# Grouped-query attention and a SwiGLU block for one decode step: K and V of two batches per load, a softmax maximum through TensorE, the FFN behind the last V, and W_O in long runs

## The chip, the cores and the metric

The kernel runs on one core of a Trainium2 chip. The core has five engines with instruction queues of their own: TensorE (PE, matmuls, with its weight loads shown as PEld), VectorE (DVE), ScalarE (ACT), GpSimd (POOL) and SyncE (SP, which here only issues transfers). They meet through semaphores. Data goes from memory (HBM) to the on-chip SBUF by DMA, split over 16 DMA engines; matmul results land in PSUM, in eight banks of 2 KB per partition.

The metric is the device time of one execution in microseconds, the median of several runs. The profile is one execution, recorded by the hardware profiler; its span runs from the first to the last instruction and is a little shorter than that run's time.

## The reference

Four sequences (B = 4), one new token each, D = 512. There are 32 query heads on 8 key/value heads (REP = 4 queries share one K and V), head size 128, and attention sees the last W = 4096 positions of a cache of 16384. All data is bf16.

```python
xn = layernorm(x)                                   # [4, 1, 512]
q  = (xn @ wq).reshape(4, 1, 32, 128)               # wq [512, 4096]
k  = repeat(k_cache[:, :, Sk - W:, :], 4, axis=1)   # cache [4, 8, 16384, 128]
v  = repeat(v_cache[:, :, Sk - W:, :], 4, axis=1)
p  = softmax(q . k * 128 ** -0.5)                   # over the 4096 positions
o  = (p . v).reshape(4, 1, 4096)
ffn = (silu(xn @ w_gate) * (xn @ w_up)) @ w_down    # [512, 1792], [512, 1792], [1792, 512]
out = x + o @ wo + ffn                              # wo [4096, 512]
```

K and V in the window are 33.6 MB each, W_Q and W_O 4.2 MB each, the three FFN weights 1.8 MB each: 81 MB that are read once.

## The kernel before

The kernel is written engine by engine: each engine's program is one list, and the order in the list is the order in which that engine works. What sets the order between engines are the semaphore waits that stand in the lists.

**Loads.** SP's list holds all large loads in one order (lines 182 to 194): W_Q in two halves, K of the first pair, W_gate, W_up, W_down, V of the first pair, then K and V of the other pairs in turn, and W_O in four pieces (`WO_CUTS`). A pair is one batch and one key/value head; there are 32. K and V of a pair are 1 MB each, laid out so that a partition holds 32 consecutive positions, which is one run of 8 KB. There are four slots for K and four for V. A load into a used slot waits until the old content has been consumed: K for the transposes (`s_tr`), V for the products with the probabilities (`s_pv`). SP waits in order, so whatever stands behind a waiting load waits too.

**Start.** ACT's queue loads x. VectorE, with ScalarE for the square and the square root, makes the layer norm (lines 217 to 226: `st_sum`, `xc`, `st_var`, `st_rstd`, `xn`). TensorE transposes xn, and makes q in 128 matmuls (line 291). GpSimd meanwhile fills constants: the identity, ones, a selection pattern, and zeros or ones in buffers that are read before they are first written (P, QT, one slot of VB), and signals `s_const` after the last of them. Then gate, up, exp, silu and down of the FFN run (lines 295 to 308), and their sum with x is kept in `y0`.

**Loop.** For each pair TensorE transposes 32 blocks of K (line 317, four groups of eight into four PSUM banks), VectorE copies each group to SBUF (`kT`, line 236), TensorE multiplies them with q to scores (line 325), ScalarE takes the exponential (line 210, with no maximum subtracted), and TensorE forms the denominators by a matmul on ones (line 335) and the products with V (line 338), which run one pair behind. VectorE reduces the denominators, inverts them and scales the output (lines 242 to 246). In TensorE's list a pair is: transposes of this pair, products with V for the pair before, scores of this pair.

**End.** The scaled outputs are permuted by matmuls on the pattern `sel` and copies (`permute`, `perm_copy`) into the layout in which W_O was loaded, in runs of 4 KB. 64 matmuls of 256 columns on W_O (line 354) add to `ps_acc`, into which y0 was put first. VectorE copies the sum to bf16, and two stores write it out.

Of the kernel before, what the change touches and what calls it, by code (L numbers as in the profile page):

```python
# [3 lines left out]
BF16 = mybir.dt.bfloat16  # L4
# [6 lines left out]
def bass_parallel_sum__sliding_block_cached__swiglu_ffn__decode_kernel(  # L11
# [18 lines left out]
    NT = W // 128  # L30
# [3 lines left out]
    NPAIR = B * HKV  # L34
    NSL = 4
    NG = 4
    KVN = NT * Dh
    PN = NT * REP
    WIDE = 64
    PS = PN + WIDE  # L40
    SCALE = float(Dh) ** -0.5
    EPS = 1e-5

# [3 lines left out]
    WQ = sb("wq_sb", [128, NC, HQ * Dh], BF16)  # L47
# [3 lines left out]
    WO = sb("wo_sb", [128, HKV, REP, D], BF16)  # L51
    KB = sb("kbuf", [128, NSL * NT * Dh], BF16)
    VB = sb("vbuf", [128, NSL * NT * Dh], BF16)
    KT = sb("kT", [128, 2 * NT * 128], BF16)
    P = sb("p", [128, 2 * PS], BF16)
    ident = sb("ident", [128, 128], BF16)
    ones = sb("ones", [128, 128], BF16)
    sel = sb("sel", [128, REP, REP, 32], BF16)
# [9 lines left out]
    QT = sb("qT", [128, HKV + 4, B, REP], BF16)  # L68
    den = sb("den", [128, REP], FP32)
    OT = sb("oT", [128, 1 + NPAIR, REP], BF16)  # L70
    OP = sb("oP", [128, REP, HKV, B], BF16)
# [4 lines left out]
    y0 = sb("y0", [B, D], FP32)  # L76
    I4w = sb("i4w", [B, 64], FP32)
# [3 lines left out]
    ps_kt = [ps("ps_kt%d" % s, [128, 512], FP32) for s in range(4)]  # L81
    ps_S = ps("ps_s", [128, 512], FP32)
    ps_O = ps("ps_o", [128, 512], FP32)
    ps_m = ps("ps_m", [128, 512], FP32)
# [3 lines left out]
    O_ps = ps_O[:, 0:REP]  # L88
    O_wide = ps_O[:, 0:WIDE]
    den_ps = ps_O[:, 128:128 + NT * REP]  # L90
    gate_ps = ps_m[:, 0:NF * B]
    up_ps = ps_m[:, 64:64 + NF * B]
    perm_ps = ps_m[:].rearrange("p (e k b h) -> p h e k b", e=REP, k=HKV, h=REP)
    q_ps = ps_acc[:, 0:HQ * B]
    down_ps = ps_acc[0:B, :]
    xT_ps = ps_m[:, 128:128 + NC * B]
# [4 lines left out]
    d_wq = [sem("d_wq%d" % h) for h in range(2)]  # L101
# [4 lines left out]
    WO_CUTS = (0, 3, 6, 7, 8)  # L106
    d_wo = [sem("d_wo%d" % q) for q in range(len(WO_CUTS) - 1)]
    s_xc = sem("s_xc")
    s_ss = sem("s_ss")
    d_k = [sem("d_k%d" % s) for s in range(NSL)]  # L110
    d_v = [sem("d_v%d" % s) for s in range(NSL)]
    s_const = sem("s_const")
# [6 lines left out]
    s_gu = sem("s_gu")  # L119
    s_ex = sem("s_ex")  # L120
    s_guT = sem("s_guT")
    s_tr = sem("s_tr")
    s_ev = sem("s_ev")
    s_sc = sem("s_sc")
    s_p = sem("s_p")
    s_pv = sem("s_pv")
    s_nrm = sem("s_nrm")
    s_pm = sem("s_pm")
    s_pc = sem("s_pc")
    s_acc = sem("s_acc")  # L130
    s_dn = sem("s_dn")
    s_y0 = sem("s_y0")
# [4 lines left out]
    wq_ap = A_wq.rearrange("(p c) n -> p c n", c=NC)  # L137
# [3 lines left out]
    wo_ap = A_wo.rearrange("(k p e) n -> p k (e n)", k=HKV, e=REP)  # L141
    ds = bass.ds

    def kv_ap(cache, i):
        return cache[i % B, i // B, Sk - W:, :].rearrange("(p t) d -> p t d", t=NT)

    with nc.Block() as block:

        @block.gpsimd
        def _(eng):  # L150
            eng.memset(ident[:], 0.0)
            eng.memset(I4[:], 0.0)
            eng.memset(I4w[:], 0.0)
            eng.memset(ones[:], 1.0)
            eng.drain()
            eng.affine_select(I4[:], I4[:], pattern=[[-1, B]], compare_op=ALU.not_equal,
                              fill=1.0, base=0, channel_multiplier=1)
            eng.affine_select(ident[:], ident[:], pattern=[[-1, 128]], compare_op=ALU.not_equal,
                              fill=1.0, base=0, channel_multiplier=1)
            eng.drain()  # L160
            eng.tensor_copy(I4w[:, 0:B], I4[:])
            for h in range(REP):
                eng.tensor_copy(sel[:, :, h, :], ident[:].rearrange("p (m e) -> p e m", e=REP))
            eng.memset(P[:], 1.0)
            eng.memset(QT[:, HKV:], 0.0)
            eng.memset(VB[:, (NSL - 1) * KVN:], 0.0).then_inc(s_const, 1)

        @block.sync
        def _(eng):
            def load_k(i):  # L170
                if i >= NSL:
                    eng.wait_ge(s_tr, NG * (i - NSL + 1))
                eng.dma_start(KB[:, i % NSL * KVN:(i % NSL + 1) * KVN].rearrange("p (t d) -> p t d", t=NT), kv_ap(A_k_cache, i)).then_inc(d_k[i % NSL], 16)  # L173

            def load_v(i):
                if i == NSL - 1:
                    eng.wait_ge(s_pv, 1)
                if i >= NSL:
                    eng.wait_ge(s_pv, i - NSL + 2)
                eng.dma_start(VB[:, i % NSL * KVN:(i % NSL + 1) * KVN].rearrange("p (t d) -> p t d", t=NT), kv_ap(A_v_cache, i)).then_inc(d_v[i % NSL], 16)  # L180

            eng.dma_start(WQ[:, 0:2], wq_ap[:, 0:2]).then_inc(d_wq[0], 16)
            eng.dma_start(WQ[:, 2:4], wq_ap[:, 2:4]).then_inc(d_wq[1], 16)
            load_k(0)
            eng.dma_start(WG[:], wg_ap).then_inc(d_wg, 16)  # L185
            eng.dma_start(WU[:], wu_ap).then_inc(d_wu, 16)
            eng.dma_start(WD[:], wd_ap).then_inc(d_wd, 16)
            load_v(0)
            for i in range(1, NPAIR):
                load_k(i)  # L190
                load_v(i)
            for n in range(len(d_wo)):
                a, b = WO_CUTS[n], WO_CUTS[n + 1]
                eng.dma_start(WO[:, a:b].rearrange("p k e n -> p k (e n)"), wo_ap[:, a:b]).then_inc(d_wo[n], 16)  # L194
# [5 lines left out]
        def _(eng):  # L200
# [5 lines left out]
            eng.wait_ge(s_gu, 1)  # L206
            eng.activation(ex[:], gate_ps.rearrange("p (t b) -> p t b", b=B), ACT.Exp, scale=-1.0).then_inc(s_ex, 1)  # L207
            for j in range(NPAIR):
                eng.wait_ge(s_sc, j + 1)
                eng.activation(P[:, j % 2 * PS:j % 2 * PS + PN], ps_S[:, 0:PN], ACT.Exp, scale=SCALE).then_inc(s_p, 1)  # L210
# [4 lines left out]
        def _(eng):  # L215

# [11 lines left out]
            eng.tensor_copy(XnT[:], xT_ps.rearrange("p (c b) -> p c b", b=B)).then_inc(s_xnT, 1)  # L228
            eng.wait_ge(s_q, 1)
            eng.tensor_copy(QT[:, 0:HKV], q_ps.rearrange("p (k h b) -> p k b h", k=HKV, b=B)).then_inc(s_nrm, 1)  # L230
            eng.engine_nop().then_inc(s_ev, 3)

            def evac(i):
                for g in range(NG):
                    eng.wait_ge(s_tr, i * NG + (g + 1))
                    eng.tensor_copy(KT[:, ds((i & 1) * KVN + 1024 * g, 1024)],  # L236
                                    kt_ps[g].rearrange("p a b -> p (a b)")).then_inc(s_ev, 1)


            def norm(j1):  # L240
                eng.wait_ge(s_pv, j1 + 1)
                eng.tensor_reduce(den[:], den_ps.rearrange("p (t h) -> p h t", h=REP), AX.X, ALU.add)  # L242
                eng.drain()
                eng.reciprocal(den[:], den[:])  # L244
                eng.drain()
                eng.tensor_tensor(OT[:].rearrange("p j h -> p (j h)")[:, ds(j1 * REP, REP)], O_ps, den[:],  # L246
                                  ALU.mult).then_inc(s_nrm, 1)

            def ffn():
                eng.wait_ge(s_ex, 1)  # L250
                eng.tensor_scalar(ex[:], ex[:], 1.0, None, ALU.add)  # L251
                eng.drain()
                eng.reciprocal(ex[:], ex[:])  # L253
                eng.drain()
                eng.tensor_tensor(gs[:], gate_ps.rearrange("p (t b) -> p t b", b=B), ex[:], ALU.mult)
                eng.drain()
# [151 lines left out]
```

## Time and profile before

| | us |
|---|---|
| median of 3 runs (lowest, highest) | 199.16 (198.95, 200.85) |
| the profiled run | 199.1 |
| its span | 197.1 |
| PE busy in the span | 150.2 |
| PE weight loads busy | 138.2 |
| DVE busy | 107.6 |
| ACT busy | 13.9 |
| POOL busy | 6.1 |
| K load, issue to landing (median of 32) | 16.2 |
| V load, issue to landing (median of 32) | 14.1 |

Busy time is a sum over instructions, and matmuls overlap in PE's pipeline, so PE's 150.2 is not time at its full rate. The page divides the span in 40 slices of 4.9 us and gives for each how busy the engines and the DMA engines were and how many GB/s moved. The time from a load's issue to its landing includes the time that it stood in the queue behind others.

### The profile page before, as it was taken

What the parts mean: (1) busy time and instruction counts of PE and PEld (TensorE: products, weight loads), DVE (VectorE), ACT (ScalarE), POOL (GpSimd) and SP (SyncE); (2) the same over time, 40 slices, a digit from 0 to 9 for tenths busy, and PEclk for the clock granted to TensorE, in tenths of its full rate; (3) what the DMA queues carried; (4) which work ended last, traced back from release to release, by engine and by line L of the source; (5) the groups of instructions that cost most, each with busy time, mean ns of one, the idle gap of its engine ahead of it and who ended that gap; (6) DMA issues with size and microseconds to landing.
All of it is one profiled execution on the core that took longest, in us unless ns stands there. A gap on an engine that the chain in (4) does not pass through costs nothing.

```text
span 197.1 us, 8105 instructions
## 1 busy us (share of the span) xinstructions
PE 150.2 (76%) x3471; PEld 138.2 (70%) x3471; DVE 107.6 (55%) x248; ACT 13.9 (7%) x39; POOL 6.1 (3%) x18
## 2 busy tenths in 40 slices
PE   0080778888888888888888888888888888888864
PEld 0080662788888878887777777877787777777742
DVE  5510001766677777666666666666666666666730
ACT  2520000001000000000000000000000000000000
POOL 8400000000000000000000000000000000000000
PEclk9999999999999999999999999999999999999999
DMA  6999999999999999999999999999999999999990
GB/s 224 429 422 433 434 424 422 426 424 426 422 422 429 427 426 429 426 427 427 429 429 431 427 426 426 427 426 429 427 426 429 426 429 426 431 429 422 418 416 37
DMA packets 11054, 81.11 MB, mean 412 GB/s; under 512 B 1180, under 2 KB 1192, under 8 KB 2216
## 3 DMA queue, kind: packets, MB, share of 16 engines
q1 hardware_dynamic: 11032, 81.01, 97.7%
q8 instruction: 6, 0.10, 0.2%
q10 hardware_dynamic: 16, 0.01, 0.0%
HBM read 81.01 MB, written 0.00 MB: 411 GB/s over the span
## 4 chain that ended last, share of the span: by engine, by line
DMA 61%; PE 26%; SPq 4%; DVE 4%; issue 3%; DVEq 0%; ACT 0%
DMA kbuf<-in_A_k_cache_dram 40%; PE ps_kt L317 13%; DMA wu_sb<-in_B_w_up_dram 11%; DMA wo_sb<-in_A_wo_dram 9%; PE ps_s L325 4%; PE ps_o L338 3%; DVE kT L236 3%; SPq L194 3%; PE ps_acc L307 2%; PE ps_m L299 2%; SPq L180 1%; PE ps_acc L354 0%; SPq L185 0%; DVE ex L253 0%; SPq L173 0%
## 5 line engine op out<-in xcount | busy, mean ns | idle before, releaser
L236 DVE COPY kT<-ps_kt 128x1024 bf16 x128 | 79.5, 683 | 45.2 <-PE ps_kt L317 45.1
L317 PE MATMUL ps_kt<-ident,kbuf 128*128 128x128 bf16 x1024 | 62.6, 219 | 6.8 <-DMA kbuf<-in_A_k_cache_dram 6.7
L317 PEld LDWEIGHTS ps_kt<-ident,kbuf 128*128 128x128 bf16 x1024 | 57.4, 98 | 9.6 <-issue 7.9
L325 PE MATMUL ps_s<-qT,kT 128*128 x1024 | 35.3, 192 | 15.8 <-DVE kT L236 15.8
L325 PEld LDWEIGHTS ps_s<-qT,kT 128*128 128x128 bf16 x1024 | 31.7, 97 | 19.4 <-issue 19.4
L338 PE MATMUL ps_o<-p,vbuf 128*128 128x64 bf16 x1056 | 36.3, 193 | 0.6 <-issue 0.6
L338 PEld LDWEIGHTS ps_o<-p,vbuf 128*128 128x128 bf16 x1056 | 34.0, 98 | 0.6 <-issue 0.6
L210 ACT ACTIVATE p<-ps_s 128x128 bf16<-128x128 f32 x32 | 8.9, 278 | 148.8 <-PE ps_s L325 148.8
L242 DVE TENSOR_REDUCE den<-ps_o 128x4 f32<-128x128 f32 x33 | 9.2, 279 | 0.9 <-PE ps_o L338 0.9
L283 PE MATMUL ps_m<-i,xn 4*128 4x4 f32 x4 | 0.6, 254 | 10.4 <-DVE xn L226 10.4
L246 DVE TENSOR_TENSOR oT<-ps_o,den 128x4 f32 (+1 forms) x33 | 5.3, 162 | 5.3 <-issue 5.2
L299 PE MATMUL ps_m<-xnT,wg_sb 128*128 128x4 bf16 x56 | 3.5, 199 | 6.2 <-DMA wg_sb<-in_B_w_gate_dram 6.2
L283 PEld LDWEIGHTS ps_m<-i,xn 4*128 4x128 f32 x4 | 0.6, 208 | 10.4 <-issue 10.4
L299 PEld LDWEIGHTS ps_m<-xnT,wg_sb 128*128 128x128 bf16 x56 | 3.4, 159 | 6.2 <-DMA wg_sb<-in_B_w_gate_dram 6.2
L251 DVE TENSOR_SCALAR ex<-ex 128x56 f32<-128x56 f32 x1 | 0.2, 191 | 13.9 <-ACT ex L207 13.9
L335 PE MATMUL ps_o<-p,ones 128*128 128x128 bf16 x33 | 7.2, 219 | 0.0
L244 DVE RECIPROCAL den<-den 128x4 f32<-128x4 f32 x33 | 5.9, 177 | 2.4
L307 PE MATMUL ps_acc<-wd_sb,guT 128*4 128x512 bf16 x14 | 4.9, 527 | 1.7 <-DVE guT L257 1.7
L354 PE MATMUL ps_acc<-wo_sb,oP 128*4 128x256 bf16 x64 | 4.2, 272 | 2.0 <-DMA wo_sb<-in_A_wo_dram 2.0
L307 PEld LDWEIGHTS ps_acc<-wd_sb,guT 128*4 128x4 bf16 x14 | 1.5, 110 | 4.7 <-issue 2.5
L354 PEld LDWEIGHTS ps_acc<-wo_sb,oP 128*4 128x4 bf16 x64 | 2.5, 84 | 3.1 <-DMA wo_sb<-in_A_wo_dram 1.6
L220 DVE TENSOR_SCALAR xc<-x_sb,st_sum 4x512 f32<-4x512 bf16 x1 | 4.4, 4381 | 0.1
(43 smaller groups left out, 36.6 us busy)
## 6 DMA issues: line engine op xcount, KB each, us to landing
kbuf<-in_A_k_cache_dram SPq DMA_DIRECT2D x32, 1024.0 KB, 16.2
vbuf<-in_A_v_cache_dram SPq DMA_DIRECT2D x32, 1024.0 KB, 14.1
wq_sb<-in_A_wq_dram SPq DMA_DIRECT2D x2, 2048.0 KB, 9.6
wo_sb<-in_A_wo_dram SPq DMA_DIRECT2D x2, 1536.0 KB, 19.1
wg_sb<-in_B_w_gate_dram SPq DMA_DIRECT2D x1, 1792.0 KB, 18.9
wu_sb<-in_B_w_up_dram SPq DMA_DIRECT2D x1, 1792.0 KB, 22.5
wd_sb<-in_B_w_down_dram SPq DMA_DIRECT2D x1, 1792.0 KB, 26.3
wo_sb<-in_A_wo_dram SPq DMA_DIRECT2D x2, 512.0 KB, 20.1
```

What stands on the lines that cost most here:

```text
L194: eng.dma_start(WO[:, a:b].rearrange("p k e n -> p k (e n)"), wo_ap[:, a:b]).then_inc(d_wo[n], 16)
L210: eng.activation(P[:, j % 2 * PS:j % 2 * PS + PN], ps_S[:, 0:PN], ACT.Exp, scale=SCALE).then_inc(s_p, 1)
L236: eng.tensor_copy(KT[:, ds((i & 1) * KVN + 1024 * g, 1024)], kt_ps[g].rearrange("p a b -> p (a b)")).then_inc(s_ev, 1)
L242: eng.tensor_reduce(den[:], den_ps.rearrange("p (t h) -> p h t", h=REP), AX.X, ALU.add)
L244: eng.reciprocal(den[:], den[:])
L299: last = mm(o[:, t * B:(t + 1) * B], w[:].rearrange("p c (m t) -> p c t m", t=NF)[:, c, t, :], XnT[:, c, :], start=(w is WG and t == 0 and ...
L307: last = mm(down_ps, guT[:, t, :], WD[:, t, :], start=(t == 0), stop=(t == NF - 1))
L317: last = eng.transpose(kt_ps[g][:, k, :], KB[:, a:a + 128], ident[:])
L325: last = mm(ps_S[:, REP * t:REP * t + WIDE], KT[:, a:a + 128], q)
L335: mm(den_ps, ones[:], P[:, p:p + PN])
L338: last = mm(O_wide, VB[:, a:a + 128], P[:, p + REP * t:p + REP * t + WIDE], start=(t == 0), stop=(t == NT - 1))
L354: last = mm(ps_acc[64 * n:64 * n + B, 0:256], OP[:, e, q, :], WO[:, q, e, 256 * n:256 * n + 256], start=False, stop=(q == HKV - 1 and e == ...
```

## The change

- K and V are loaded for two batches of one key/value head at once: 16 loads of 2 MB each in place of 32 of 1 MB. A partition holds 64 consecutive positions of one batch, a run of 16 KB; even partitions belong to the one batch and odd ones to the other. There are two slots each in place of four.
- Scores of both batches are computed together, eight columns per block. A matmul of rank two (`mask`) puts -1e30 where a partition and a column belong to different batches.
- A maximum is subtracted: VectorE reduces the scores over the blocks (`row_max`), TensorE transposes that (`max_rows`), VectorE reduces it and puts it on a diagonal (`shift`), and a matmul adds it, negated, to all 512 columns of scores. The exponential follows that.
- In TensorE's list an iteration is now: first half of the transposes, transposed maximum of the iteration before, second half of the V products of two iterations before, first half of the scores, shift, second half of the transposes, first half of the V products of the iteration before, second half of the scores.
- W_Q is one load. W_down stays early; W_gate and W_up come behind the last V, and the whole FFN runs there. Its down product, x and W_O add up in the same PSUM bank, without y0.
- W_O is loaded with 32 rows per partition, in pieces of 16, 10, 4 and 2 KB per partition. The outputs are brought into that layout by four transposes, a copy and four matmuls on a pattern `rep`.
- Constants change with all that: GpSimd clears more buffers, among them three quarters of VB in place of a quarter, and signals `s_const` in two steps.

```diff
+    ND = B * HKV // 2
+    C = 2 * REP
+    NT = 2 * W // 128
+    HT = NT // 2
...
-    wo_ap = A_wo.rearrange("(k p e) n -> p k (e n)", k=HKV, e=REP)
+    wo_ap = A_wo.rearrange("(p c) n -> p c n", c=NO)
...
-    def kv_ap(cache, i):
-        return cache[i % B, i // B, Sk - W:, :].rearrange("(p t) d -> p t d", t=NT)
+    def kv_ap(cache, d):
+        b0 = d % 2 * 2
+        return cache[b0:b0 + 2, d // 2, Sk - W:, :].rearrange("b (q t) d -> q b (t d)", t=NT)
...
+            eng.memset(QZ[:], 0.0)
+            eng.drain()
+            eng.engine_nop().then_inc(s_const, 1)
             eng.memset(P[:], 1.0)
-            eng.memset(QT[:, HKV:], 0.0)
-            eng.memset(VB[:, (NSL - 1) * KVN:], 0.0).then_inc(s_const, 1)
+            eng.memset(VB[:, HKN:], 0.0)
+            eng.drain()
+            eng.engine_nop().then_inc(s_const, 1)
+            eng.engine_nop().then_inc(d_v[1], 16)
...
+            def load_k(d):
+                if d >= 2:
+                    eng.wait_ge(s_tr, 2 * NG * (d - 1))
+                eng.dma_start(KB[:, d % 2 * KVN:(d % 2 + 1) * KVN], kv_ap(A_k_cache, d)).then_inc(d_k[d % 2], 16)
+
+            def load_v(d):
+                eng.wait_ge(s_pv, d + 1)
+                eng.dma_start(VB[:, d % 2 * KVN:(d % 2 + 1) * KVN], kv_ap(A_v_cache, d)).then_inc(d_v[d % 2], 16)
+
+            eng.dma_start(WQ[:], wq_ap).then_inc(d_wq, 16)
             load_k(0)
+            load_k(1)
+            eng.dma_start(WD[:], wd_ap).then_inc(d_wd, 16)
+            load_v(0)
+            for d in range(2, ND):
+                load_k(d)
+                load_v(d - 1)
+            load_v(ND - 1)
             eng.dma_start(WG[:], wg_ap).then_inc(d_wg, 16)
             eng.dma_start(WU[:], wu_ap).then_inc(d_wu, 16)
...
+            with eng.Fori(0, ND // 2) as r:
+                for b in range(2):
+                    row_max(1 - b, 2 * r + (b + 1))
+                    evac(0, 4 * NG * r + 2 * NG * b)
+                    shift(2 * r + (b + 1))
+                    norm(2 * r + (b + 1), b, r)
+                    evac(1, 4 * NG * r + (2 * NG * b + NG))
...
+            def mask(bank):
+                return mm(ps_S[bank][:].rearrange("p (t c) -> p t c", c=C), mkr[:],
+                          mkc[:].rearrange("j (o c) -> j o c", o=1).to_broadcast([2, NT, C]), start=True)
...
+            def shift(bank, n):
+                eng.wait_ge(s_dg, n)
+                mm(ps_S[bank][:].rearrange("p (t c) -> p t c", c=C), ones[0:C, :],
+                   Dg[:].rearrange("j (o c) -> j o c", o=1).to_broadcast([C, NT, C])).then_inc(s_sh, 1)
...
+            eng.wait_ge(s_const, 2)
+            eng.wait_ge(s_qz, 1)
+            mm(ps_O[:, 0:256], ones[:], P[:, 0:256], start=True)
+            mask(1).then_inc(s_sc, 1)
...
+                    eng.wait_ge(d_k[b], r * 16 + 16)
+                    transposes(0, ev, b)
+                    max_rows(n)
+                    pv(b, 1, n)
+                    scores(0, ev, b, q)
+                    shift(1 - b, n)
+                    transposes(1, ev + NG, b)
+                    pv(1 - b, 0, (r * 16 + 16, n))
+                    scores(1, ev + NG, b, q)
+            max_rows(ND + 1)
+            pv(0, 1, ND + 1)
+            shift(1, ND + 1)
...
+            pv(1, 0, (8 * ND + 16, ND + 1))
+            pv(1, 1, None)
+            up_gate(WG, gate_ps, s_gate, d_wg)
...
+            up_gate(WU, up_ps, s_up, d_wu)
+            for n in range(2):
+                mm(ps_acc[64 * n:64 * n + 64, 0:256], I4w[:], X[:, 256 * n:256 * n + 256], start=True)
             eng.wait_ge(s_guT, 1)
             eng.wait_ge(d_wd, 16)
             for t in range(NF):
...
+                for n in range(2):
+                    mm(ps_acc[64 * n:64 * n + B, 0:256], guT[:, t, :], WD[:, t, 256 * n:256 * n + 256])
+            eng.wait_ge(s_op, 1)
+            for c in range(NO):
+                if c in WO_CUTS:
+                    eng.wait_ge(d_wo[WO_CUTS.index(c)], 16)
+                for n in range(2):
+                    last = mm(ps_acc[64 * n:64 * n + B, 0:256], OP[:, c, :], WO[:, c, 256 * n:256 * n + 256])
             last.then_inc(s_acc, 1)
```

More of the change, by code (lines that the diff above doesn't have):

```diff
@@ L100, in bass_parallel_sum__sliding_block_cached__swiglu_ffn__decode_kernel @@
     d_x = sem("d_x")
[L101 removed]
+    d_wq = sem("d_wq")
     d_wg = sem("d_wg")
@@ L245, in norm @@
                 eng.drain()
[L246 to L256, printed above, removed]
-                eng.tensor_tensor(guT[:], up_ps.rearrange("p (t b) -> p t b", b=B), gs[:], ALU.mult).then_inc(s_guT, 1)
```

330 lines of the change are left out of this document (172 added, 158 removed).

## The prediction

> **What bounds the kernel now.** I read the page from the top: the slices and the queue first, then the chain, then windows of single stages, then the timeline at both ends.
>
> ```profile
> span 197.1 us, 8105 instructions
> ...
> DMA  6999999999999999999999999999999999999990
> GB/s 224 429 422 433 434 424 422 426 424 426 422 422 429 427 426 429 426 427 427 429 429 431 427 426 426 427 426 429 427 426 429 426 429 426 431 429 422 418 416 37
> ...
> q1 hardware_dynamic: 11032, 81.01, 97.7%
> ...
> DMA 61%; PE 26%; SPq 4%; DVE 4%; issue 3%; DVEq 0%; ACT 0%
> ```
>
> The 16 DMA engines are busy in every slice but the two ends, and 81 MB pass at a rate that hardly moves. No compute engine does that. So the kernel is a stream: it ends when the last byte has landed and a short tail of matmuls, a copy and a store is done. The chain of waits gives PE 26%, from a stretch in which PE catches up, but no slice of the DMA row shows a hole for it. The profiled time is 199.1 us, 2.0 over its span, and agrees with the median of 199.16. A change can gain by a higher rate, and loses by any hole in the stream or by a longer tail.
>
> **Longer runs.** Stages by windows: from 4 us W_Q (16 KB runs), from 18.5 the FFN weights (14 KB), from 30 K and V (8 KB), from 181 mostly W_O (4 KB); the last row counts what has passed by 26.4 us.
>
> ```profile
> 3.00:12.00 9.00, 1.29 (x29) 1.23 (x30) 5.24 (x5) 3.49 (x5) 4.02 (x4) 1.00 1.01 431
> 18.50:22.50 4.00, 1.45 (x24) 1.45 (x25) 0.00 (x0) 0.00 (x0) 0.00 (x0) 1.00 1.02 437
> 30.00:180.00 150.00, 127.65 (x2989) 118.42 (x2989) 93.97 (x217) 8.33 (x30) 0.00 (x0) 1.00 1.01 427
> 181.00:192.00 11.00, 8.46 (x189) 6.88 (x186) 5.42 (x19) 0.55 (x2) 0.00 (x0) 1.00 1.02 419
> 0.00:26.40 26.40, 8.81 (x207) 8.59 (x207) 6.29 (x7) 4.77 (x6) 6.07 (x18) 1.00 0.94 391
> ```
>
> K and V are 64 x 1.049 = 67.1 MB. At 427 GB/s they take 157.2 us, at the 431 of the 16 KB runs 155.7: -1.5. W_O (4.19 MB, now 16, 10, 4 and 2 KB runs) goes from 419 to about 431: -0.3. Together **-1.8**; at worst 0 (runs from two batches could fetch no better than those from one), at best -4.0 (437 for all of it). I take 431, the row whose run is equally long.
>
> **The start: a longer memset.** The page's queue part shows nothing here; the timeline does.
>
> ```profile
> 0.74 0.56 ACTq L201 DMA_DIRECT2D x_sb<-in_A_x_dram  x1
> 2.16 0.67 DVE L218 TENSOR_REDUCE st_sum<-x_sb 4x1 f32<-4x512 bf16 x1 [2.16 <-DMA x_sb<-in_A_x_dram]
> 2.91 4.38 DVE L220 TENSOR_SCALAR xc<-x_sb,st_sum 4x512 f32<-4x512 bf16 x1
> 3.07 0.41 POOL L164 MEMSET p<- 128x384 bf16 x1
> 3.43 0.14 POOL L165 MEMSET qT<- 128x64 bf16 x1
> 3.52 3.50 POOL L166 MEMSET vbuf<- 128x4096 bf16 x1
> 7.33 0.63 ACT L203 ACTIVATE xsq<-xc 4x512 f32<-4x512 f32 x1 [4.71 <-DVE xc L220]
> 9.82 0.47 DVE L226 TENSOR_SCALAR xn<-xc,st_rstd 4x512 f32<-4x512 f32 x1
> 11.32 3.57 PE L291 MATMUL ps_acc<-xnT,wq_sb 128*128 128x4 bf16 x128 [0.27 <-DVE xnT L228]
> 14.93 0.29 DVE L230 CAST qT<-ps_acc 128x128 bf16<-128x128 f32 x1 [3.67 <-PE ps_acc L291]
> ```
>
> xc takes 4.38 us where xn, of the same size, takes 0.47, and it ends at 7.29, 0.27 after GpSimd's memset of vbuf ends at 7.02. VectorE sat behind GpSimd. xn came later and was free. Before, that hid behind W_Q, which lands at about 12.
>
> The change makes this memset 12288 columns wide: at 3.50 us for 4096, 10.5. In front of it come more small memsets and selects, a memset of 1024 columns and P's of 1152 (0.41 for 384). I add them at these prices, with gaps at the two drains, and reach about 6.4 for its start and **16.9** for its end. xc should slip in at the drain ahead of P, at about 5, but xn, due at 8 to 9, meets the long memset. Then xn ends at 17.2 (+0.27, as xc did); W_Q's matmuls start 1.03 later (10.29 to 11.32), run 3.6, and the two QZ copies take 0.45 (one of twice the size took 0.29): 22.3. The matmul on ones and the mask (256 and 512 columns) come first in the loop's queue, so the first transpose starts at about S = **22.9**.
>
> The order of the queue makes that count. SP loads W_Q, K0, K1 and W_D freely (10.2 MB; 391 GB/s x 26.4 us = 10.3, so it runs dry at **26.3**), then waits for the first pv, a dummy, before V0. Every later load and the output's weights are queued behind that wait. The dummy comes after 32 transposes, and those are likely slow:
>
> ```profile
> 25.29 3.52 PE L299 MATMUL ps_m<-xnT,wu_sb 128*128 128x4 bf16 x56 [0.72 <-DMA wu_sb<-in_B_w_up_dram]
> 30.50 4.91 PE L307 MATMUL ps_acc<-wd_sb,guT 128*4 128x512 bf16 x14 [1.69 <-DVE guT L257]
> 30.88 0.13 PEld L307 LDWEIGHTS ps_acc<-wd_sb,guT 128*4 128x4 bf16 x1 [0.30 <-issue]
> 31.31 0.13 PEld L307 LDWEIGHTS ps_acc<-wd_sb,guT 128*4 128x4 bf16 x1 [0.30 <-issue]
> 34.17 0.73 PEld L307 LDWEIGHTS ps_acc<-wd_sb,guT 128*4 128x4 bf16 x4 [0.17 <-issue]
> ```
>
> The first W_D matmuls are 0.43 us apart, or 0.83 ns a column, until about 34; then 0.2, although the granted clock reads 1.00 all along. 4-column matmuls ahead of them had not brought PE up to speed. After W_Q's matmuls the same holds: 32 x 128 columns x 0.83 ns = 3.4 us, the dummy 0.94 to 1.7 (I take 1.3), 0.2 for the semaphores: 27.8. From issue to data the x load shows 1.4 (0.74 to 2.16): V0 flows from 29.2. The hole is **+2.9**; with PE fast from the start +1.0, with every step slow +3.6.
>
> **The loop.** One iteration now does two batches. Its price comes from a stretch where the old loop ran on PE and VectorE alone:
>
> ```profile
> 44.17 1.95 PE L317 MATMUL ps_kt<-ident,kbuf 128*128 128x128 bf16 x32
> 44.37 0.28 ACT L210 ACTIVATE p<-ps_s 128x128 bf16<-128x128 f32 x1 [4.12 <-PE ps_s L325]
> 45.00 2.48 DVE L236 COPY kT<-ps_kt 128x1024 bf16 x4 [1.13 <-PE ps_kt L317]
> 46.01 1.10 PE L338 MATMUL ps_o<-p,vbuf 128*128 128x64 bf16 x32
> 47.40 0.28 DVE L242 TENSOR_REDUCE den<-ps_o 128x4 f32<-128x128 f32 x1
> 47.61 1.10 PE L325 MATMUL ps_s<-qT,kT 128*128 x32 [0.51 <-DVE kT L236]
> 48.09 0.16 DVE L246 TENSOR_TENSOR oT<-ps_o,den 128x4 f32 x1 [0.16 <-issue]
> 48.55 0.56 PE L317 MATMUL ps_kt<-ident,kbuf 128*128 128x128 bf16 x7
> ```
>
> A unit is 0.83 to the first copy, 2.48 for four copies, 0.13, and 0.94 of scores: 4.38. An iteration has two. First half: the maximum is a reduce of 512, like x's 0.67, and runs where VectorE waited 0.83 for the first transposes; it pushes the copies by about 0.12. Its transpose and the mask lie in PE's wait for the copies. Second half: the shift matmul (512 columns, 0.23 at full speed) stands bare between scores and transposes; the exponential of 512 (like the 0.63 of xsq) lies under the transposes; the normalisation, once in place of twice, under 0.83 + 0.23. With 0.05 for loop instructions, 2 x 4.38 + 0.12 + 0.23 + 0.05 = **9.15 us**. The stream needs 4.194 MB / 431 = 9.73. So the loop keeps up: cost 0. Of the loads behind SP's waits, a K is issued 6.6 into the iteration before last (after its transposes) and a V 3.0 into its own, and each then has over 5 us of stream ahead of it; that two slots of 2 MB stand for four of 1 MB costs nothing while this holds. That gate and up follow V15 moves bytes in the queue and adds none. The reserve is small: K15 has landed at S + 6.3 + 28 transfers of 4.87 = S + 142.6; PE is ready for it at S + 2.5 (slow first iteration) + 15 c. Above c = 9.34 each 0.1 us costs 1.5. V15 follows V14 directly and waits for iteration 15: 1.8 + 0.94 + 0.3, and 1.4 to data, is 4.5 after K15; V14 covers 4.87.
>
> **The end.** Gate, up and down now follow the last V, with W_O's 64 matmuls behind them.
>
> ```profile
> 191.70 1.91 PE L354 MATMUL ps_acc<-wo_sb,oP 128*4 128x256 bf16 x32 [1.32 <-DMA wo_sb<-in_A_wo_dram]
> 194.24 0.60 PE L354 MATMUL ps_acc<-wo_sb,oP 128*4 128x256 bf16 x8 [0.63 <-DMA wo_sb<-in_A_wo_dram]
> 194.88 0.42 DVE L275 CAST y_sb<-ps_acc 128x256 bf16<-128x256 f32 x1 [4.71 <-PE ps_acc L354]
> ```
>
> The stream ends at 194.1 - 1.8 + 2.9 = 195.2. W_U landed 9.7 before that (4.19 MB), at 185.5, and K15 18.3 before W_U, at 167.2. From there PE needs 9.15 for iteration 15; 3.2 for maximum, pv, shift and exponential; 2.15 for the last two pv halves; 3.5 for gate; 1.3 for the transposes, the copy and the permutation: 186.6. Up 3.5, guT 0.45, W_D 28 matmuls in pairs, slow as in the rows above (14 x 0.213 = 3.0), W_O 2 slow pairs and 30 at 1.91/16: 4.0. PE ends at 197.6, where 194.86 - 1.8 + 2.9 = 196.0 would be the stream's. **+1.6**, at least -0.3 (a shorter last piece) if PE is fast.
>
> The Trainium skill (TensorE: Matmul & The Clock Gate, Part 1) says PE slows only after an idle window of about 3.4 us; PE has no such pause between pv and W_D, so W_D would run fast and the sum be some 1.5 lower. In the trace W_D is slow with no longer pause than 1.7 us ahead of it, but PE had not been fast before, so it decides only half of this.
>
> **Sum.** 199.1 - 1.8 + 2.9 + 1.6 = **201.8 us**.
>
> **Rivals.** *Both VectorE steps are held.* xc waited through P's, qT's and vbuf's memsets without getting in; if a drain lets it in no better, xc too ends at 17.2, xn 3.0 later (7.29 to 10.29), and S, the hole and the end move by 3.0: 204.8. The Trainium skill (SBUF — State Buffer, Who interferes with whom) says that whichever of GpSimd and such a VectorE operation starts first holds the port for that instruction only. By that, xc would have got in at 3.5; here it did not, so the rule does not exclude this rival.
>
> *The loop is the bound.* If the maximum's reduce or the shift is dearer (a reduce of 1.1 us), c = 9.6 and V15 waits 15 x 0.26 = 3.9 more: 205.7. Against it: the den reduce, strided too, costs 0.28 for 128, the price of a plain one.
>
> *The other side: no hole.* If the long memset does not hold xn, S is 17 to 18 (memset, and K0's landing). Below S = 20.0, V0 is in the queue before 26.3, and the hole is gone. With PE fast in the tail, the sum is 199.1 - 1.8 - 0.3 = 197.0; with a rate between 431 and 437, 196. For it: one held instruction is all the evidence there is. Against: its 4.38.
>
> **How the numbers follow.** Forecast 0.45, both held 0.18, loop-bound 0.14, no hole 0.23 (half of it with the slow tail, about 199). What a measurement can tell from no change is about 1%: 197.2 to 201.2. Faster: half of the no-hole case, 0.12. Same: its other half and the part of the forecast with PE fast in one place, 0.30. Slower: the rest, 0.58. The range 197.8 to 205.2 leaves out the best of the no-hole case and the worst of the loop-bound one. The forecast's own range is 199.5 to 203.
>
> **What would show it.** Right: xc short or ending near 5 to 6, xn ending just behind a vbuf memset of 10.5 us; one hole in the DMA row at 26 to 29, SP waiting for PE in it; loop iterations paced by K's landing at 9.7; W_O landed before PE reaches it. Wrong: xn before 12, no hole, or SP waiting on PE throughout, or a last matmul that waits for W_O.

## The result and the profile after

| | before | after |
|---|---|---|
| median, us (lowest, highest) | 199.1 (198.95, 200.85) | 205.94 (204.29, 206.33) |
| ratio to before | | 1.031, 95% interval 1.023 to 1.039 |
| the profiled run, us | 199.1 | 206.33 |
| its span, us | 197.1 | 204.4 |

The change costs 3.1%, by the ratio of the runs' means. The direction was forecast; the size, 201.8 with a range up to 205.2, was too small. The profiled run is the slowest of the four. K0 to K15 and V0 to V15 below are the 16 loads of each, in order.

From the page of the changed kernel: the span, the granted clock, the DMA engines in 40 slices of 5.1 us, the main queue and the chain that ended last.

```profile
span 204.4 us, 8087 instructions
...
PEclk9999999999999999999999999999999999988559
DMA  7989928999999999999999999999999997899980
GB/s 257 449 385 439 419 85 366 427 406 443 414 443 430 417 446 420 446 427 420 446 417 449 423 427 439 417 449 423 433 436 417 446 423 337 314 422 435 423 358 8
...
q1 hardware_dynamic: 5768, 81.01, 93.6%
...
DMA 43%; PE 43%; DVE 9%; issue 2%; ACT 1%; DVEq 0%
```

Before, no slice but the first and the last was under 9 in the DMA row. Now there are two marks in it. Slice 6 (25.6 to 30.7 us) moves 85 GB/s and slice 7 starts late: a hole. Slices 34 and 35 (from 169 us) move 337 and 314: a dip. The PEclk row says that TensorE's clock fell near the end, which the row of the kernel before does not show. The chain has lost 18 points of DMA and gained 17 of PE.

The start, from the timeline (start, duration, what ran, and in brackets the idle time before it with its releaser):

```profile
3.01 1.46 DVE L255 TENSOR_SCALAR xc<-x_sb,st_sum 4x512 f32<-4x512 bf16 x1
3.53 1.50 POOL L191 TENSOR_SCALAR_AFFINE_SELECT mkr<-mkr 2x128 bf16<-2x128 bf16 x1
6.23 1.06 POOL L200 MEMSET p<- 128x1152 bf16 x1
7.00 10.84 DVE L261 TENSOR_SCALAR xn<-xc,st_rstd 4x512 f32<-4x512 f32 x1
7.22 10.35 POOL L201 MEMSET vbuf<- 128x12288 bf16 x1
18.87 3.57 PE L331 MATMUL ps_acc<-xnT,wq_sb 128*128 128x4 bf16 x128 [0.27 <-DVE xnT L263]
23.89 3.59 PE L357 MATMUL ps_kt<-ident,kbuf 128*128 128x128 bf16 x32
29.20 0.54 SPq L215 DMA_DIRECT2D vbuf<-in_A_v_cache_dram  x1
```

xc ended at 4.47, while GpSimd's select of `mkr` ran (3.53 to 5.03). xn did not get through like that: it ended at 17.84, 0.27 behind the memset that ends at 17.57. The first transposes start at 23.9 and V0 is issued at 29.20.

Windows of the hole, of the loop and of the dip (busy time of PE, PEld, DVE, ACT and POOL, then granted clock, DMA share and GB/s):

```profile
26.00:27.00 1.00, 1.00 (x12) 1.00 (x11) 0.84 (x2) 0.00 (x0) 0.00 (x0) 1.00 0.18 72
27.00:28.00 1.00, 1.00 (x14) 0.69 (x13) 0.84 (x2) 0.00 (x0) 0.00 (x0) 1.00 0.03 14
28.00:29.00 1.00, 1.00 (x29) 1.00 (x26) 0.62 (x3) 0.00 (x0) 0.00 (x0) 1.00 0.00 0
29.00:30.00 1.00, 1.00 (x27) 0.72 (x24) 0.54 (x3) 0.00 (x0) 0.00 (x0) 1.00 0.06 16
30.00:31.00 1.00, 1.00 (x23) 0.72 (x20) 0.13 (x1) 0.12 (x1) 0.00 (x0) 1.00 0.71 131
31.00:32.00 1.00, 1.00 (x22) 1.00 (x19) 0.57 (x1) 0.47 (x1) 0.00 (x0) 1.00 0.74 279
32.00:33.00 1.00, 1.00 (x26) 1.00 (x23) 1.00 (x3) 0.00 (x0) 0.00 (x0) 1.00 0.91 377
...
60.00:160.00 100.00, 91.53 (x2059) 82.00 (x2056) 67.94 (x143) 5.97 (x10) 0.00 (x0) 1.00 1.01 432
...
172.00:173.00 1.00, 1.00 (x34) 0.95 (x33) 1.00 (x3) 0.00 (x0) 0.00 (x0) 1.00 0.43 180
173.00:174.00 1.00, 1.00 (x28) 0.77 (x26) 0.85 (x5) 0.00 (x0) 0.00 (x0) 1.00 0.12 49
174.00:175.00 1.00, 1.00 (x22) 0.72 (x19) 0.17 (x2) 0.23 (x1) 0.00 (x0) 1.00 0.71 131
175.00:176.00 1.00, 1.00 (x22) 1.00 (x20) 0.67 (x2) 0.37 (x1) 0.00 (x0) 1.00 0.96 360
```

At 430 GB/s the seven rows from 26 to 33 us should have moved 3010 us x GB/s; they moved 889. That is 2121 / 430 = 4.9 us of stream. The four rows from 172 us miss 1000 / 430 = 2.3 us in the same way. In between the rate is the forecast one, 432.

The granted clock of 1.00 in the rows ahead of 28.6 us is no measurement. The trace's clock records begin there (at 34.0 in the kernel before), and a window without a record is printed as 1.00. The matmuls tell more: 32 transposes took 3.59 us there and 1.96 at 169.92.

The end, from the timeline:

```profile
169.92 1.96 PE L357 MATMUL ps_kt<-ident,kbuf 128*128 128x128 bf16 x32 [0.76 <-DMA kbuf<-in_A_k_cache_dram]
173.09 0.54 SPq L215 DMA_DIRECT2D vbuf<-in_A_v_cache_dram  x1
182.25 3.58 PE L331 MATMUL ps_o<-p,vbuf 128*128 128x64 bf16 x64
185.66 3.49 PE L331 MATMUL ps_kt<-xnT,wg_sb 128*128 128x4 bf16 x56
190.74 3.52 PE L331 MATMUL ps_kt<-xnT,wu_sb 128*128 128x4 bf16 x56
194.64 3.15 PE L331 MATMUL ps_acc<-wd_sb,guT 128*4 128x256 bf16 x28
197.58 4.51 PE L331 MATMUL ps_acc<-wo_sb,oP 128*4 128x256 bf16 x64
202.13 0.42 DVE L326 CAST y_sb<-ps_acc 128x256 bf16<-128x256 f32 x1 [7.54 <-PE ps_acc L331]
```

And the granted clock there, by windows:

```profile
182.20:185.60 3.40, 3.40 (x67) 3.40 (x65) 0.00 (x0) 0.00 (x0) 0.00 (x0) 0.51 1.02 434
185.60:189.00 3.40, 3.40 (x61) 3.40 (x58) 0.66 (x3) 0.00 (x0) 0.00 (x0) 0.99 1.03 434
189.10:199.30 10.20, 9.67 (x113) 7.08 (x114) 1.82 (x6) 0.22 (x1) 0.00 (x0) 0.50 0.93 388
```

The last W_O piece has landed at 200.4. W_O's matmuls do not wait for it: from K15's transposes on, nothing on PE waits for a transfer by more than 0.2 us. So this run's end is K15's landing plus PE's own work. The forecast had K15 at 167.2 and PE's end 30.4 later; the trace has 169.9 and 32.2. These two differences, 2.7 and 1.8, are the 4.5 us by which the profiled run exceeds 201.8; the median exceeds it by 4.1.

### The profile page after: what moved, and what is told of

It is laid out like the page before. It is cut to its first block, busy times and chain, and to the rows that moved or that the text cites. A ratio compares the mean times of both kernels' runs of the same rounds, so it can differ in the third digit from the quotient of the medians.

```text
span 204.4 us, 8087 instructions
## 1 busy us (share of the span) xinstructions
PE 171.0 (84%) x3634; PEld 151.5 (74%) x3634; DVE 124.9 (61%) x248; ACT 15.1 (7%) x24; POOL 16.6 (8%) x22
## 4 chain that ended last, share of the span: by engine, by line
DMA 43%; PE 43%; DVE 9%; issue 2%; ACT 1%; DVEq 0%
DMA kbuf<-in_A_k_cache_dram 43%; PE ps_kt L357 16%; PE ps_s L331 9%; PE ps_o L331 7%; PE ps_acc L331 6%; DVE xn L261 5%; PE ps_kt L331 4%; DVE kT L276 1%; DVE xc L255 1%; DMA x_sb<-in_A_x_dram 1%; ACT L241 1%; ACT xsq L239 0%; DVE rm L281 0%; DVE st_sum L253 0%; PE ps_acc L336 0%
## 5 line engine op out<-in xcount | busy, mean ns | idle before, releaser
L276 DVE COPY kT<-ps_kt 128x1024 bf16<-128x1024 bf16 x128 | 79.8, 684 | 24.5 <-PE ps_kt L357 24.5
L357 PEld LDWEIGHTS ps_kt<-ident,kbuf 128*128 128x128 bf16 x1024 | 58.8, 99 | 14.1 <-issue 14.0
L331 PEld LDWEIGHTS ps_s<-qz,kT 128*128 128x128 bf16 x1024 | 31.4, 98 | 6.9 <-issue 3.6
L331 PE MATMUL ps_s<-qz,kT 128*128 x1024 | 34.7, 192 | 1.3
L281 DVE TENSOR_REDUCE rm<-ps_s 128x8 bf16<-128x512 f32 x17 | 11.8, 692 | 19.6 <-PE ps_s L331 19.6
L244 ACT ACTIVATE p<-ps_s 128x512 bf16<-128x512 f32 x17 | 10.2, 597 | 163.7 <-PE ps_s L331 163.7
L261 DVE TENSOR_SCALAR xn<-xc,st_rstd 4x512 f32<-4x512 f32 x1 | 10.8, 10841 | 0.1
L201 POOL MEMSET vbuf<- 128x12288 bf16 x1 | 10.3, 10348 | 0.0
L331 PE MATMUL ps_o<-p,ones 128*128 128x128 bf16 (+1 forms) x69 | 7.0, 222 | 1.3 <-ACT p L244 0.7
L331 PE MATMUL ps_s<-mkc,mkr 2*128 2x512 bf16 x17 | 6.8, 398 | 0.0
L331 PE MATMUL ps_s<-dg,ones 8*128 8x512 bf16 x17 | 6.5, 385 | 0.0
## 6 DMA issues: line engine op xcount, KB each, us to landing
wd_sb<-in_B_w_down_dram SPq DMA_DIRECT2D x1, 1792.0 KB, 25.6
```

The lines of the kernel that those rows point to most:

```text
L201: eng.memset(VB[:, HKN:], 0.0)
L244: eng.activation(P[:, d % 2 * PS:d % 2 * PS + SN], ps_S[d % 2][:], ACT.Exp, scale=SCALE).then_inc(s_p, 1)
L261: eng.tensor_scalar(xn[:], xc[:], st_rstd[:, 0:1], None, ALU.mult).then_inc(s_xn, 1)
L276: eng.tensor_copy(KT[:, u * HKN + 1024 * g:u * HKN + 1024 * (g + 1)], kt_ps[g].rearrange("p a b -> p (a b)")).then_inc(s_ev, 1)
L281: eng.tensor_reduce(RM[:], ps_S[bank][:].rearrange("p (t c) -> p c t", c=C), AX.X, ALU.max).then_inc(s_rm, 1)
L331: return eng.matmul(o, l, r, start=start, stop=stop, skip_group_check=True)
```

## The experiments

All edits are made to the changed kernel. Their runs of the kernel before had medians of 199.05 to 199.23.

**The start.** Two ways to free xn: a memset of half the duration (the same bytes as half as many 32-bit elements), and the long memset placed behind xn.

```diff
-            eng.memset(VB[:, HKN:], 0.0)
+            eng.memset(VB[:, HKN:].bitcast(FP32), 0.0)
```

> The long memset of vbuf written as 6144 fp32 columns of zeros, the same bytes, so that it should take 5.2 us in place of 10.35 and end at about 12.4. Theory A (the memset holds VectorE's xn, and that holds the first V load): xn ends at 12.7, the first transpose stands at 18.7 in place of 23.9, V0 is issued near 24, and the hole of the stream at 26 to 30 is gone; K15 lands 4 us earlier and the end comes 4 us earlier: about 202. Theory B (the hole only lets the slower DMA engines catch up, so that it costs less than its width): the hole is gone but K15 lands only 2 to 2.5 us earlier: about 203.5. Rival C (the memset takes the same time per byte, not per column): it still takes 10.3 and nothing changes: 206.

```diff
+            eng.wait_ge(s_xn, 1)
             eng.memset(VB[:, HKN:], 0.0)
```

> GpSimd waits for xn before the same long memset (12288 columns, 10.35 us). Theory A (VectorE's xn is held by the memset): xn takes 0.5 us and ends near 7.5; W_Q's matmuls wait for W_Q alone (landing near 13) and end near 16.6; the loop then waits for the constants, near 18, so the first transpose stands at 18.5 to 19 and the time is as with the half memset, 202 to 203.5. Rival (xn is slow for another reason, or the start is held by the constants and not by xn): xn still takes over 10 us, or the first transpose stays near 24: 206.

Measured: 200.97 us, ratio 1.009 (1.006 to 1.013), and 201.46 us, ratio 1.012 (1.008 to 1.017). The timelines, first with the short memset:

```profile
7.00 5.72 DVE L261 TENSOR_SCALAR xn<-xc,st_rstd 4x512 f32<-4x512 f32 x1
7.22 5.23 POOL L201 MEMSET vbuf<- 128x6144 f32 x1
18.77 1.46 PE L357 MATMUL ps_kt<-ident,kbuf 128*128 128x128 bf16 x12
```

then with the long one behind xn:

```profile
7.00 0.56 DVE L262 TENSOR_SCALAR xn<-xc,st_rstd 4x512 f32<-4x512 f32 x1
7.62 10.34 POOL L202 MEMSET vbuf<- 128x12288 bf16 x1 [0.33 <-DVE xn L262]
19.01 1.25 PE L358 MATMUL ps_kt<-ident,kbuf 128*128 128x128 bf16 x10
```

xn ends 0.27 us behind the memset beside it: after 10.84 us, after 5.72, or after 0.56 where only P's memset (until 7.29) is beside it. In both versions the transposes start 5 us earlier and the hole is gone; the first version moves 360 to 423 GB/s in every 2 us window from 24 to 32. The medians differ by 205.94 - 200.97 = 5.0 us, near the 4.9 counted in the windows; the ratios give 4.2, within 1.8 either way. K15 landed at 164.5 in place of 169.8. So the first theory of the expectation holds, with a larger gain than the 4 us it named. The second version shows it without touching the memset: the memset still takes 10.34 and nothing is lost to it but 0.2 us of start, since the loop's first matmul now waits for it.

**The last V.** V15 is loaded into the space of W_Q, which is dead by then, so that it waits for nothing late.

```diff
-            load_v(ND - 1)
+            eng.wait_ge(s_q, 1)
+            eng.dma_start(WQ[:, 0:KVN], kv_ap(A_v_cache, ND - 1)).then_inc(d_vl, 16)
...
-            pv(1, 0, (8 * ND + 16, ND + 1))
-            pv(1, 1, None)
+            pv(1, 0, (16, ND + 1), WQ, 0)
+            pv(1, 1, None, WQ, 0)
```

> The last V goes into W_Q's place in SBUF, which is free by then, with no wait for a product; its products read it there. The dip of the stream at 172 to 175 should be gone and the last W_O piece should land 1.5 to 2 us earlier (near 198.5). Theory A (behind K15, TensorE's own chain sets the end, 32 us from K15's landing to the last matmul): the time falls by 0 to 0.4 us: 205.5 to 206. Rival (the stream sets the end): it falls by 1.7 or more: 204 or less.

**The clock.** Three matmuls of 512 columns in each of PE's two pauses ahead of the last products with V, so that PE is not idle there.

```diff
+            fill(3)
             max_rows(ND + 1)
...
+            fill(3)
             pv(1, 0, (8 * ND + 16, ND + 1))
```

> Six matmuls of 512 columns into an unused PSUM bank, three in each of the two places where TensorE waits behind the loop (for the last maximum, and for the last exponential), so that the granted clock should not fall to 0.5 at 182. They take about 0.7 us in each of two waits of 0.8 and 0.7 us, so they cost next to nothing. Theory A (TensorE's chain sets the end, and 1.3 us of it is that the last 68 V products run at half clock): those products take 2.2 in place of 3.6 us and the end comes 1.0 to 1.4 us earlier, until W_U's landing holds it: about 205. Rival (the clock falls anyway, by what TensorE did earlier): no change, or 0.2 us more: 206. If the stream sets the end: no change either, with the products faster.

Measured for the last V: 204.35 us, ratio 1.026 (1.017 to 1.034), in two groups: spans of 201.0 and 201.2 at a mean granted clock of 0.983, and of 204.0 and more at 0.967. In the profiled run, one of the first group, the dip is gone:

```profile
172.00:176.00 4.00, 4.00 (x90) 3.44 (x86) 2.70 (x9) 0.60 (x1) 0.00 (x0) 1.00 1.04 446
```

There the last products with V happened to run at the full clock (2.03 us, where the changed kernel took 3.58). So the time of this run alone can't tell the dip from the clock. At the same mean clock, 0.967, its spans are 204.0 and 204.4, and the changed kernel's two are 204.4: there, in two runs each, the dip was worth next to nothing, as the first theory said. Measured for the fills: 206.59 us, ratio 1.036 (1.032 to 1.039), no gain. The timeline of that run:

```profile
183.38 2.03 PE L331 MATMUL ps_o<-p,vbuf 128*128 128x64 bf16 x64
186.48 3.52 PE L331 MATMUL ps_kt<-xnT,wg_sb 128*128 128x4 bf16 x56 [1.07 <-DMA wg_sb<-in_B_w_gate_dram]
191.94 3.52 PE L331 MATMUL ps_kt<-xnT,wu_sb 128*128 128x4 bf16 x56 [0.29 <-DMA wu_sb<-in_B_w_up_dram]
```

The products did get fast, and PE then waited for W_gate and W_up, which the dip had delayed; in this run K15 also landed 1.1 later, at 170.9. So two paths end almost together in the changed kernel: PE at half clock, and W_up behind V15. Mending one of them alone shows the other.

**Start and last V together.** The short memset and V15 without its wait:

> The half memset and the last V without a wait, together. Both holes should be gone, and the last W_O piece should land near 193.7 (195.2 with the half memset alone, less the 1.5 that V15's restart cost). From K15's last landing (164.5) TensorE's chain took 29.1 us with the last V products at full clock and 32.0 at half clock. Theory A (what is left is TensorE's chain behind K15): last matmul at 193.6 to 196.5, time 198 to 200.5, around the kernel before or a little above. Rival (the two holes overlap in what they cost, so that closing the second returns nothing): 201, as with the half memset alone.

Measured: 200.31 us, ratio 1.006 (1.002 to 1.009). That is 0.7 us under the short memset alone, and the two intervals overlap: the trace shows that the dip is gone, the times only that it was worth between nothing and some 1.7 us (0.0094 - 0.0055, with the two intervals' half-widths combined, by 199). Its end, from the timeline:

```profile
177.76 2.03 PE L333 MATMUL ps_o<-p,wq_sb 128*128 128x64 bf16 x64
...
191.33 4.91 PE L333 MATMUL ps_acc<-wo_sb,oP 128*4 128x256 bf16 x64
```

The last W_O piece has landed at 193.4, PE ends at 196.2. This version is the base of the next five.

**The maximum.** Without `row_max`, `max_rows` and `shift`; the exponential follows the scores. This leaves out the softmax maximum, which the kernel before did not subtract either.

> As e5_both, without the maximum: no reduce over the blocks, no transpose of it, no second reduce and no shift matmul; the exponential takes the masked scores as they are. Theory A (the loop waits for K and V, so the maximum costs nothing in it, and only the last one stands in the chain behind K15: 0.7 reduce, 0.2 matmul, 0.3 shift): K still lands every 9.7 us, and the end comes 0.5 to 1.2 us earlier than e5_both. Rival (the maximum costs 0.4 us or more in each of 16 iterations): 5 us earlier or more.

Measured: 199.96 us, ratio 1.002 (0.999 to 1.005). From the list of waits, PE's wait for K over the whole run (total, times, longest):

```profile
PE ps_kt L355 <- DMA kbuf<-in_A_k_cache_dram: 17.1, 13, 2.2
```

With the maximum that total is 9.6. The stream keeps its 431 GB/s. The maximum fills time in which PE would wait; the medians differ by 0.35 us, and the intervals overlap.

**The runs.** Each load of K and V as two loads of half the columns, so that a partition's run is 8 KB, as in the kernel before.

```diff
-                eng.dma_start(KB[:, d % 2 * KVN:(d % 2 + 1) * KVN], kv_ap(A_k_cache, d)).then_inc(d_k[d % 2], 16)
+                halves(eng, KB[:, d % 2 * KVN:(d % 2 + 1) * KVN], A_k_cache, d, (d_k[d % 2], d_kb[d % 2]))
```

> As e5_both, but each load of K or V is issued as two loads of half its columns, so that runs are 8 KB again and loads are 1 MB. Theory A (the longer runs are worth 1.5 us of stream): the rate in the loop falls from 430 to 432 GB/s to 427, K15 lands 1.2 to 1.6 us later, and the time rises by as much, to 199.5 to 202. Rival (run length is worth nothing): the same time within 0.4. Other rival (runs from two batches cost something whatever their length): the rate falls below 427.

Measured: 201.22 us, ratio 1.011 (1.005 to 1.016). The window of the loop:

```profile
60.00:160.00 100.00, 91.19 (x2026) 81.70 (x2024) 67.76 (x143) 5.97 (x10) 0.00 (x0) 1.00 1.01 427
```

This is the 427 GB/s of the kernel before. By the medians the long runs of K and V are worth 0.9 us here, with intervals that overlap; by K15's landing, at 167.4 in place of 165.3, they are worth 2.1.

**The clock in the FFN.** 14 matmuls of 512 columns among those of gate and up.

> As e5_both, with one matmul of 512 columns into an unused PSUM bank before every second group of four gate and up matmuls (14 in all), to see whether the granted clock falls because those 4-column matmuls leave the array idle. It adds 14 x 0.22 = 3.1 us to the chain (6 if the clock stays at half). Theory A (it falls for lack of columns): the clock stays at 1.0 through W_D and W_O, W_D takes 1.7 in place of 3.1 and W_O 3.9 in place of 4.5; net about 1 us slower than e5_both. Rival (the clock falls whatever TensorE does there, or 14 matmuls are too few): W_D and W_O stay slow, and the time is 3 to 6 us above e5_both.

Measured: 203.1 us, ratio 1.019 (1.013 to 1.026). Two windows from gate to W_O:

```profile
182.90:185.60 2.70, 2.13 (x29) 1.79 (x28) 0.45 (x2) 0.22 (x1) 0.00 (x0) 1.00 1.06 454
185.80:195.80 10.00, 9.73 (x98) 6.60 (x99) 1.22 (x4) 0.00 (x0) 0.00 (x0) 0.50 0.60 249
```

The clock fell all the same and the fills cost 2.8 us. How much work would hold it up is not known from this.

**The FFN.** First without its computation but with all loads; then back in front of the loop, with gate and up behind W_Q and the down product behind the first iteration (`iteration` is the body of TensorE's loop, `down` the matmuls on x and W_down).

> The version with the cheap memset and the unconstrained last V, its FFN left out of the computation: the matmuls of gate, up and down and the SiLU are gone, all loads stay, so the output lacks the FFN term. It shows the stream alone. If the tail behind the last V is what stands above the stream (in that version the last W_O piece landed at 193.4 us of the span and the last matmul ended at about 196.2), the last matmul now ends 0.6 to 0.9 behind the last W_O piece, at about 194.1, and the time falls by about 2 us, from 200.3 to 198.2. Rival: the stream itself ends later than that piece suggests, or W_O's matmuls are slow whatever stands ahead of them and start no earlier; then the time falls by under 1 us.

> The same version with the FFN put back in front: W_gate and W_up are loaded behind W_Q and ahead of K0, gate, up and SiLU run before the loop, the down product behind the first iteration, and its sum with x waits in SBUF as in the kernel before. Nothing is left out. Behind the last V only the permutation and W_O stand. If the tail of the FFN is the cost, K15 lands 8.5 us later than before (3.67 MB at 431 GB/s: 165.3 + 8.5 = 173.8), the last products with V end some 14.3 behind that, at about 188, W_O's matmuls start at 189.5 to 190 and the last ends at 194.2 with its last piece: 198.3 us, 2 us less than with the FFN behind V15 and just below the kernel before. Rival: the attention's own end (K15 to the last product, 14.3 us) now sticks out, as its W_O matmuls run at half clock and take 4.9: last matmul 195 or later, 199 to 200. Second rival: the 3.1 us of the down product inside the loop are not made up, the stream stalls, and the time is 200 or more.

```diff
             eng.dma_start(WQ[:], wq_ap).then_inc(d_wq, 16)
+            eng.dma_start(WG[:], wg_ap).then_inc(d_wg, 16)
+            eng.dma_start(WU[:], wu_ap).then_inc(d_wu, 16)
             load_k(0)
...
+            iteration(0, 0)
+            down()
+            iteration(0, 1)
+            with eng.Fori(1, ND // 2) as r:
+                for b in range(2):
+                    iteration(r, b)
```

Measured without the FFN's computation: 197.69 us, ratio 0.993 (0.990 to 0.995), so 2.6 us under the same version with it: most of what stands above the stream is the tail of the FFN. Here W_O waits for its first piece, as the last line of PE's timeline shows:

```profile
188.73 6.56 PE L322 MATMUL ps_acc<-wo_sb,oP 128*4 128x256 bf16 x64 [4.65 <-DMA wo_sb<-in_A_wo_dram]
```

This profiled run, 199.29, is the slowest of its six. Its clock was at 0.50 from 184.5 to 194.7, and W_O ended 1.75 behind its last piece (193.54) and not the 0.6 to 0.9 expected: slow W_O matmuls do not need the FFN ahead of them.

Measured with the FFN in front: 201.31 us, ratio 1.012 (1.010 to 1.013), 1.0 us worse than behind V15. Two windows of its stream fall short:

```profile
44.00:46.00 2.00, 2.00 (x48) 1.72 (x45) 0.97 (x5) 0.60 (x1) 0.00 (x0) 1.00 0.85 295
54.00:58.00 4.00, 4.00 (x91) 3.60 (x87) 2.62 (x5) 0.60 (x1) 0.00 (x0) 1.00 0.94 320
```

They miss 0.6 and 1.0 us: the down product delays PE, PE delays V1's and V2's issue, and the queue runs short. V0 was issued 8.6 us later than in the base version, as the two loads ahead explain; V1 10.6 and V2 11.5. Of V2's extra delay, 0.7 is a pause of PE that the trace gives no reason for. The second rival of the expectation, then. Of the first rival the outcome came with it, the attention's own end stands out, but not its half clock (first line: the down product, for below):

```profile
38.58 1.69 PE L342 MATMUL ps_acc<-wd_sb,guT 128*4 128x256 bf16 x28
...
190.94 0.40 PE L460 MATMUL ps_kt<-ident,oT 128*32 128x128 bf16 x4 [0.90 <-DVE oT L309]
192.77 3.66 PE L342 MATMUL ps_acc<-wo_sb,oP 128*4 128x256 bf16 x64 [0.53 <-DVE oP L335]
```

Even at full clock, 2.9 us pass between the last product, which ended at 189.9, and W_O, because normalising and permuting now have no gate and up beside them. No version that computes everything beats the kernel before; the one that leaves the FFN's computation out, 0.7% under it, shows how little is left.

## Why the prediction was right in direction and too small

**The longer runs (-1.8): right in the rate.** 432 GB/s in the loop for a forecast 431, and 427 with the runs cut again. For the runs of K and V the forecast gave 1.5; the runs without them show 0.9 by time and 2.1 by K15's landing. W_O's 0.3 did not come: it moved at 419 GB/s (188.7 to 197.2), and before the same stretch of bytes moved at 420 (182.4 to 191.0).

**xc slips in, xn is held: right, xc partly by luck.** xc ended at 4.47, during a select, and not at the drain ahead of P, which the forecast counted on. xn ended at 17.84 for a forecast 17.2. The rival that both are held is out by xc, the one without a hole by the windows. The Trainium skill (SBUF — State Buffer, Who interferes with whom) gives the shared port to whichever of VectorE and GpSimd starts first. xn's record starts at 7.00, ahead of the long memset's 7.22, while P's memset still ran to 7.29, and yet it came last; with nothing behind P's memset it was done at 7.56. The trace doesn't bear the rule out for an instruction that is already waiting.

**The hole (+2.9): mis-sized, 4.9 us.** The queue ran dry at about 26.2, as forecast (26.3). Two steps behind that were too short. V0's issue came at 29.20, not 27.8: 0.7 from the memset, which ended at 17.57 and not at 16.9, 0.3 more up to the first transposes (S 23.9 for 22.9), and 0.4 between them and the issue (5.3 for 4.9). The transposes themselves took 3.6 for 3.4, as slow as forecast. The puzzle in that step, slow matmuls at a granted clock of 1.00 "all along", is the reading of windows without a clock record: W_D turned fast in the kernel before at about 34, where the records begin. And "1.4 from issue to data", taken from x's load of 4 KB, is not how an empty queue starts again: the windows show 131, 279 and 377 GB/s in the three microseconds from 30, which equals a full stream from 31.2, 2.0 after the issue. 1.4 + 0.6 is the missing 2.0.

**The loop (0): right.** K paces it at 9.72 us per load, PE waits for K in 13 of 16 iterations (8.8 us in all), and the maximum is hidden.

**V15 (0): wrong as a step.** "V14 covers 4.87" took a load as one event. The landing records of the 16 DMA engines (us) say otherwise:

```
         first    half   last engine
K15     167.85  168.16  169.80
V14     172.69  172.99  174.61
```

PE starts only when the last engine is done (169.92), but half of the queue runs ahead of it by 1.6 us or more. V15, issued 3.3 behind K15's landing, came when half of the engines had been out of work for 0.1 us or more, and they then had to start again. In the kernel before, the same spread is about 2.0 us, but there the queue held more than one load: a load took 14.1 to 16.2 us from issue to landing, where its own 1 MB takes 2.5 at 427 GB/s. The dip is real, 2.3 us by the windows; without it the changed kernel was not surely faster, and where the clock fell as here PE ended as late.

The same lag shows in the loop's own figure for K15, S + 142.6 = 165.5, which is also 1.7 under the 167.2 that the end was worked out from. With the measured restart it gives 31.2 + 136.4 = 167.6. The first engine's part landed then (167.85), the last one's 2.0 later.

**The end (+1.6): the mechanism right, PE's chain mis-sized by 1.8.** Iteration 15 took 9.05 for 9.15 and maximum and exponential 3.05 for 3.2. The last products with V took 3.6 to the gate for 2.15, at half clock, which the prediction did not see. It is not fixed by the kernel, it seems: two of the four runs have a mean clock of 0.975 in place of 0.967, which is some 3.4 us less at half clock, and one of them is the fastest, 204.29. W_D took 2.9 to the first of W_O for 3.0, and W_O 4.55 for 4.0. The rest, 0.4, is in the transposes and the permutation. The forecast that W_D would be slow was right, and for a measured reason: the granted clock was 0.50 from 189.1 to 199.3. The Trainium skill (TensorE: Matmul & The Clock Gate, Part 1) lets the clock fall after an idle window of about 3.4 us; here PE is busy in all of 185.6 to 189.0, with 4-column matmuls, and the clock falls behind that. The trace doesn't agree with the rule as it is worded. What sets the clock is not settled by these runs. Against the stream's own end the overhang is 202.1 - 200.4 = 1.7 in this run, 2.8 in the version with both mends, and 2.6 by the run without the FFN.

**In sum.** K15 came 2.7 late, and PE's chain behind it ran 1.8 long. Of the 2.7, 2.0 is the hole. Some 0.4 more is that the longer runs had returned less by then: summed over the traces' DMA packets, the changed kernel is 4.9 us behind the one before when 12 MB have passed, and 3.9 when 68.9 MB have, at about K15's end. That is 1.0 returned where the forecast has about 1.4 up to there. The other 0.3 is open; the spread of K15's parts alone varies from 1.5 to 2.7 between the profiled runs that load K in one piece.

The failed step is the size of the hole, **+2.9** by "V0 flows from 29.2", which was 31.2: V0 was issued 1.4 late, and the empty queue took 0.6 longer to come back. The experiments on the start show that this hole is paid for in time, 4.2 to 5.0 us. The second step is "2.15 for the last two pv halves", counted at full clock, which took 3.6 at half. Of the rivals' prices, "no hole, with the slow tail, about 199" can be held against the version with the short memset, 201.0: the tail was too cheap there by the same cause, and V15's dip was still in it.

## What to carry to other kernels

A clearing instruction on GpSimd can hold a VectorE instruction that has nothing to do with it for all of its own duration: put long ones behind the last small step that others wait for. Count a load that waits on compute from the time when the queue in front of it is empty on most engines, not from when the loads before it are complete, and add some 2 us from its issue (as here) if the queue does run dry. Work that is moved behind the last V costs what outlasts the stream, here 1.7 to 2.8 us, and behind many 4-column matmuls it can run at half of TensorE's clock.

## What the runs showed of the hardware

- GpSimd's memset goes by elements, not by bytes: 12288 bf16 columns take 10.35 us, the same bytes as 6144 f32 columns 5.23.
- The granted clock changed in steps of 3.4 us or multiples of it. It fell to 0.5 behind a step in which PE was busy with 4-column matmuls, and also behind one in which three matmuls of 512 columns stood among them (PE busy 2.9 of 3.45 us). The same 28 W_D matmuls took 3.15 us in the tail and 1.69 behind the first iteration, where wider matmuls preceded them.
- One load's parts land some 2.0 us apart on the 16 engines in steady state, in both kernels. After V15's restart the spread was 0.7. What makes an engine lag was not tried.
